# PSUM's eight banks shared out as three, three and two in place of four, two and two, in a Fourier and maxout kernel

## The chip, the cores and the metric

The kernel runs on one core of a Trainium2 chip. The metric is the device time of one execution in microseconds (us); lower is better. The kernel before was run three times; the profile is of one more execution, taken by the hardware profiler. Engines are named as the profile does: PE (TensorE), DVE (VectorE), ACT (ScalarE), POOL (GpSimd) and SP (SyncE, which here issues DMAs).

## The reference

A Fourier transform along the sequence, a complex matrix product, a soft threshold, the inverse transform, and then a layer that takes the largest of three products per token.

```python
def _attn_ref(x, w_r, w_i, b_r, b_i):            # x: (8, 3072, 256)
    X = np.fft.rfft(x, axis=1)
    Yr = X.real @ w_r - X.imag @ w_i + b_r
    Yi = X.real @ w_i + X.imag @ w_r + b_i
    Yr = np.sign(Yr) * np.maximum(np.abs(Yr) - 0.01, 0.0)
    Yi = np.sign(Yi) * np.maximum(np.abs(Yi) - 0.01, 0.0)
    return np.fft.irfft(Yr + 1j * Yi, n=3072, axis=1)

def _moe_ref(x, w1, w2, w3, w_out):              # x: (24576, 256), w1..w3: (256, 768)
    h = np.maximum(np.maximum(x @ w1, x @ w2), x @ w3)
    return h @ w_out                              # (24576, 256)
```

## The kernel before

**Precision.** A float32 operand is held as two float16 halves, high and low, and a product is three float16 matmuls into the same PSUM tile (`mm3`, lines 132, 133 and 134). Batch 0 alone goes through the Fourier part in float32.

**The Fourier part of a batch** turns 3072 points into 48 x 64. `stage_a` (L437) makes two PSUM tiles `pa`, which ACT copies out (L439) and a DMA writes to DRAM (`a_d`). After a reload (`aj`), `stage_b` makes one tile `px` per step; ACT and DVE read it (L127, L552, L553). `stage_w1` and `stage_w2` make one tile `py` each, the product with the complex weights, read by ACT (L631) and DVE (L620). `stage_q` makes `pz`, which ACT copies (L675) and a DMA writes to DRAM (`z_d`). Each of these steps is done 12 times per batch, `stage_a` 8 times.

**The inverse** of a chunk of 384 tokens (`inverse`, L735) reads `z_d` back and makes two tiles `pi`, which ACT and DVE split into the halves `yh` and `yl` (L127).

**The layer** works chunk by chunk (8 chunks per batch) and in six steps `f` per chunk. The weights are rearranged so that only two up products are needed: `up` makes two PSUM tiles `pu` of 128 x 384, each from six matmuls; ACT takes the ReLU of the first (`c`, L757), DVE the larger of that and the second (`h`, L759), and ACT and DVE split it into the halves of `hh` (L127). `down` (lines 132 to 134 into `pd`, from `hh`) multiplies by the output weights, nine matmuls per step. The part of the third product goes in through a product of weights (`wsh`, `wsl`). Two tiles `pd` take the sums of all six steps; ACT copies them out (L786).

**The order of the work.** The main loop at the end of `fourier_maxout_kernel` issues `up(f)`, then `down` of the step before, then what `run_until` has due of the next batch's Fourier part; with `f == 4` comes `inverse` of the next chunk. So PE's order around any step is: two tiles `pu`, `down` of the step before, some Fourier tiles, two tiles `pu`, and so on. PE, ACT and DVE each take their instructions in the order in which they stand. A scheduler may move instructions when the program is built: it knows how many buffers each pool has.

**PSUM.** It has eight banks, and each PSUM tile is one bank. A tag names a pool of banks: a new tile with the tag can be written when an earlier tile of the tag has been read for the last time. Before, `ff` had four banks, `up` two and `dn` two. All Fourier, inverse and small tiles come from `ff_tile`; from the main loop on, they all have the tag `ff` (`spare` is cut to one entry). Before the main loop, when no up or down products run, `ff_tile` takes tags from the list `spare` in turn, so that all eight banks serve the Fourier part of batch 0. `pu` has the tag `up` (L749) and `pd` the tag `dn`.

Of the kernel before, what the change touches and what calls it, by code (L numbers as in the profile page):

```python
# [9 lines left out]
F32 = mybir.dt.float32  # L10
# [86 lines left out]
def fourier_maxout_kernel(  # L97
# [5 lines left out]
    P = 128  # L103
# [14 lines left out]
    ps = ctx.enter_context(tc.tile_pool(name="ps", bufs=3, space=PSUM))  # L118
# [6 lines left out]
    def split_scaled(hi, lo, src, scale):  # L125
        h = hi if hi.dtype == F16 else hi.bitcast(F32)
        return nc.scalar.activation(out=hi, in_=src, func=AF.Copy, scale=scale), nc.vector.scalar_tensor_tensor(  # L127
            out=lo, in0=src, scalar=scale, in1=h, op0=ALU.mult, op1=ALU.subtract
        )

    def mm3(o, lh, ll, rh, rl, start=True, stop=True, **kw):
        nc.tensor.matmul(o, lh, rh, start=start, stop=False, **kw)  # L132
        nc.tensor.matmul(o, lh, rl, start=False, stop=False, **kw)  # L133
        nc.tensor.matmul(o, ll, rh, start=False, stop=stop, **kw)  # L134


    spare = ["ff", "up", "ff", "dn"]

    def ff_tile(name):
        tag = spare[0]  # L140
        if len(spare) > 1:
            spare.append(spare.pop(0))
        return ps.tile([P, 512], F32, name=name, tag=tag, bufs=4 if tag == "ff" else 2)

    fr = const.tile([XR, 64], F32, name="fr")
    qf = const.tile([P, 2, P], F32, name="qf")
# [50 lines left out]
    def exponent_of(mx, name, bits, mask, low):  # L197
        rows = mx.shape[0]
        col = small("col", bufs=2)
        nc.vector.tensor_reduce(out=col[0:rows], in_=mx, axis=AX.X, op=ALU.max)  # L200
        pt = ff_tile("pt")
        nc.tensor.matmul(
            pt[:, 0:rows], col[0:rows].broadcast_to([rows, P]), id_sb[0:rows, 0:rows],
            start=True, stop=True,
        )
        e = small("e" + name, U32, 2)
        nc.vector.tensor_reduce(out=e.bitcast(F32), in_=pt[:, 0:rows], axis=AX.X, op=ALU.max)
        nc.vector.tensor_scalar(
            out=e, in0=e, scalar1=bits, scalar2=mask, op0=ALU.logical_shift_right, op1=ALU.bitwise_and
        )  # L210
        nc.vector.tensor_scalar(out=e, in0=e, scalar1=low, scalar2=None, op0=ALU.max)
        return e
# [53 lines left out]
    class Weights:  # L266
# [27 lines left out]
        def phases(self, n):  # L294
# [32 lines left out]
            def turn():  # L327
                pt = ff_tile("pt")
                for j in range(width // P):
                    for v, first in ((m, True), (r, False)):  # L330
                        nc.tensor.matmul(
                            pt[:, j * P:j * P + P], v[:, j * P:j * P + P], id_sb, start=first, stop=not first
                        )
                pv = pt[:, 0:width].rearrange("p (f d) -> p f d", d=P)
                nc.scalar.activation(out=hi, in_=pv, func=AF.Copy)
                nc.vector.tensor_tensor(out=lo, in0=pv, in1=hi, op=ALU.subtract)
# [24 lines left out]
    def straight():  # L361
        ps_m = ff_tile("pm")
        for kd in range(KD):
            for f in range(NF):
                lh, ll = (t[:, f, kd * P:kd * P + P] for t in (wth, wtl))
                mm3(ps_m[:, kd * D:kd * D + D], lh, ll, woh[:, f], wol[:, f], start=f == 0, stop=f == NF - 1)
        split_scaled(*(t.rearrange("p k d -> p (k d)") for t in (wsh, wsl)), ps_m, H_SCALE)
# [320 lines left out]
    for q in range(NCH + 2, NB * NCH):  # L688
        b, i = divmod(q, NCH)
        p = i if b == 1 else (b - 2) * SLOTS + NF * i + 2  # L690
# [3 lines left out]
    for b in range(1, NB):  # L694
        for k in range(-2, NJP + 1):
            p = 8 + 2.2 * (k + 2) if b == 1 else (b - 1) * SLOTS + 2.8 * (k + 2)
# [49 lines left out]
    def up(y, f):  # L746
        pu = []
        for i in range(2):
            p = ps.tile([P, 512], F32, name="pu", tag="up", bufs=2)  # L749
            for kd in range(KD):  # L750
                mm3(
                    p[:, 0:NT], wuh[:, i, kd, f * P:(f + 1) * P], wul[:, i, kd, f * P:(f + 1) * P],
                    y[0][:, kd], y[1][:, kd], start=kd == 0, stop=kd == KD - 1,
                )
            pu.append(p[:, 0:NT])
        c1 = ffn.tile([P, NT], F32, name="c1")
        nc.scalar.activation(out=c1, in_=pu[0], func=AF.Relu)  # L757
        h32 = ffn.tile([P, NT], F32, name="h32")
        nc.vector.tensor_tensor(out=h32, in0=pu[1], in1=c1, op=ALU.max)  # L759
        hh = ffn.tile([P, 2, NT], F16, name="hh", bufs=4)  # L760
        st["hh"] = split_scaled(hh[:, 0], hh[:, 1], h32, H_SCALE)
        return hh
# [94 lines left out]
    for b in range(NB):  # L857
        for c in range(NCH):
            nxt = (b, c + 1) if c + 1 < NCH else (b + 1, 0) if b + 1 < NB else None
            for f in range(NF):  # L860
                hh = up(y, f)
                if prev:
                    down(*prev)
                prev = (b, c, f, hh, y)
                if b == c == 0:
                    for _ in range(5):
                        pump()
                    if f == 2:
                        split_fft_weights(fft_weights)
                    if f == 4:  # L870
                        straight()
                    if f in (3, 5):
                        for i in (f - 3, f - 2):
                            load_blocks(i)
                if nxt and f == 4:
                    y_next = inverse(*nxt)
                run_until(b * SLOTS + c * NF + f)
                if nxt and f == 1:
                    load_z(*nxt)
                    behind = st["hh"]  # L880
                if nxt and f == 3:
                    with tc.issue_after(behind[0].ins), tc.issue_after(behind[1].ins):
                        split_z(nxt[0])
            y = y_next
# [34 lines left out]
```

## Time and profile before

| | |
|---|---|
| three runs | 1828.95, 1829.1 and 1826.92 us; median 1828.95 us |
| profiled execution | 1830.64 us, of which the span from first to last instruction is 1828.8 us |
| busy over the span | PE 97%, DVE 71%, ACT 52%, POOL 7% |
| granted TensorE clock, mean | 0.997 |
| PE busy, 0 to 46 us | 22.7 us |
| PE busy, 46 to 200 us | 136.4 of 154 us |
| PE busy, 200 to 1829 us | 197 to 199 of every 200 us, 223.3 of the last 229 us |

The 0.0 of all times is the first instruction. Up to about 135 us the kernel loads and does the Fourier part of batch 0 while the weights are split; then the layer runs for 64 chunks, beside the Fourier part of the batch after. A row of the timeline gives start, duration, engine, line, operation and tiles (out<-in), and in brackets how long the engine was idle before and what ended that. Matmuls are pipelined: a `pu` matmul starts 0.16 us after the one before it, but its row says 0.33 us, and a `pd` matmul starts after 0.11 us and its row says 0.27 us. So idle time counts from an end that lies about 0.16 us behind the start of the next possible matmul, and a short wait shows no idle time at all.

### The profile page before, as it was taken

What the parts mean: (1) busy time and instruction counts of PE and PEld (TensorE: products, weight loads), DVE (VectorE), ACT (ScalarE), POOL (GpSimd) and SP (SyncE); (2) the same over time, 40 slices, a digit from 0 to 9 for tenths busy, and PEclk for the clock granted to TensorE, in tenths of its full rate; (3) what the DMA queues carried; (4) which work ended last, traced back from release to release, by engine and by line L of the source; (5) the groups of instructions that cost most, each with busy time, mean ns of one, the idle gap of its engine ahead of it and who ended that gap; (6) DMA issues with size and microseconds to landing.
All of it is one profiled execution on the core that took longest, in us unless ns stands there. A gap on an engine that the chain in (4) does not pass through costs nothing.

```text
span 1828.8 us, 39424 instructions
## 1 busy us (share of the span) xinstructions
PE 1766.7 (97%) x16071; PEld 1259.3 (69%) x16071; DVE 1303.5 (71%) x2580; ACT 954.6 (52%) x1930; POOL 130.1 (7%) x183
## 2 busy tenths in 40 slices
PE   4979999999999999999999999999999999999999
PEld 2755677767676777667677677766766677777776
DVE  1897789767886688757886588866888568864443
ACT  2335565555554556455554565545555455544443
POOL 0001100100000000100001000010001000000000
PEclk9999999999999999999999999999999999999999
DMA  8634433233323232232322333223232212211110
GB/s 247 221 116 120 126 93 88 72 111 91 94 66 103 86 94 84 69 117 77 96 82 70 113 90 91 78 70 115 86 96 67 87 53 73 64 36 54 40 36 27
DMA packets 116600, 164.71 MB, mean 90 GB/s; under 512 B 13137, under 2 KB 88914, under 8 KB 116418
## 3 DMA queue, kind: packets, MB, share of 16 engines
q1 hardware_dynamic: 54466, 86.66, 16.7%
q10 hardware_dynamic: 61952, 75.52, 13.6%
q8 instruction: 126, 2.06, 0.5%
q14 instruction: 56, 0.46, 0.1%
HBM read 86.64 MB, written 75.50 MB: 89 GB/s over the span
## 4 chain that ended last, share of the span: by engine, by line
PE 67%; DVE 13%; ACT 7%; DMA 6%; issue 4%; ACTq 2%; SPq 1%; POOL 0%; DVEq 0%; POOLq 0%
PE pu L132 10%; PE pu L134 10%; PE pu L133 10%; PE pd L134 7%; PE pd L133 6%; PE pd L132 6%; PE pa L437 3%; DVE u L620 3%; DVE h L759 2%; PE pi L735 2%; PE py L132 2%; PE py L134 2%; PE py L133 2%; DMA aj<-a_d 2%; ACTq L787 2%
## 5 line engine op out<-in xcount | busy, mean ns | idle before, releaser
L132 PE MATMUL pu<-yh,wuh 128*128 128x384 f16 x1536 | 501.5, 327 | 13.0 <-DVE h L759 7.1
L134 PE MATMUL pu<-yh,wul 128*128 128x384 f16 x1536 | 500.9, 326 | 0.0
L133 PE MATMUL pu<-yl,wuh 128*128 128x384 f16 x1536 | 500.8, 326 | 0.0
L127 ACT ACTIVATE hh<-h 128x384 f16<-128x384 f32 x384 | 200.6, 522 | 383.7 <-DVE h L759 376.2
L759 DVE TENSOR_TENSOR h<-pu,c 128x384 f32<-128x384 f32 x384 | 212.9, 554 | 162.5 <-PE pu L134 87.9
L134 PE MATMUL pd<-woh,hh 128*128 128x256 f16 x1152 | 313.9, 273 | 4.2 <-DVE hh L127 4.2
L132 PE MATMUL pd<-woh,hh 128*128 128x256 f16 x1152 | 313.9, 273 | 0.9 <-ACT hh L127 0.6
L133 PE MATMUL pd<-wol,hh 128*128 128x256 f16 x1152 | 313.9, 273 | 0.0
L127 DVE SCALAR_TENSOR_TENSOR hh<-h,hh 128x384 f16<-128x384 f32 x384 | 213.6, 556 | 122.0 <-ACT hh L127 120.8
L757 ACT ACTIVATE c<-pu 128x384 f32<-128x384 f32 x384 | 187.0, 487 | 129.4 <-PE pu L134 120.8
L132 PEld LDWEIGHTS <-wuh 128*128 128x128 f16 x1536 | 150.2, 98 | 115.0 <-issue 32.5
L133 PEld LDWEIGHTS <-wuh 128*128 128x128 f16 x1536 | 150.1, 98 | 102.4 <-issue 20.9
L134 PEld LDWEIGHTS <-wul 128*128 128x128 f16 x1536 | 150.1, 98 | 99.3
L620 DVE SCALAR_TENSOR_TENSOR u<-py,s1x,cs 64x256 f32<-64x256 f32 x308 | 148.4, 482 | 40.3 <-ACT cs L631 35.7
L132 PE MATMUL py<-wch,tt 128*128 128x256 f16 x504 | 137.7, 273 | 0.0
L134 PE MATMUL py<-wch,tt 128*128 128x256 f16 x504 | 137.4, 273 | 0.0
L133 PE MATMUL py<-wcl,tt 128*128 128x256 f16 x504 | 137.4, 273 | 0.0
L711 POOL MEMSET zp<- 32x1024 f32 x64 | 60.3, 943 | 1073.2 <-DVE zl L127 1029.4
L133 PEld LDWEIGHTS <-hh 128*128 128x128 f16 x1152 | 112.6, 98 | 31.5 <-issue 1.6
L132 PEld LDWEIGHTS <-hh 128*128 128x128 f16 x1152 | 112.7, 98 | 30.5 <-ACT hh L127 1.0
L134 PEld LDWEIGHTS <-hh 128*128 128x128 f16 x1152 | 112.6, 98 | 24.2 <-DVE hh L127 9.6
L786 ACT ACTIVATE o<-pd,s1u 128x256 f32<-128x256 f32 x192 | 83.1, 466 | 62.0 <-PE pu L134 35.4
(184 smaller groups left out, 2936.2 us busy)
## 6 DMA issues: line engine op xcount, KB each, us to landing
aj<-a_d SPq DMA_DIRECT2D x96, 256.0 KB, 2.8
z_d<-zs ACTq DMA_DIRECT2D x96, 256.0 KB, 2.2
zp<-z_d SPq DMA_DIRECT2D x128, 192.0 KB, 3.0
out_dram<-o ACTq DMA_DIRECT2D x192, 128.0 KB, 2.3
a_d<-aq ACTq DMA_DIRECT2D x124, 192.0 KB, 3.1
xq<-in_x_dram SPq DMA_DIRECT2D x120, 192.0 KB, 3.3
rw<-in_moe_w_dram SPq DMA_DIRECT2D x12, 384.0 KB, 7.5
xr<-in_x_dram SPq DMA_DIRECT2D x16, 96.0 KB, 3.8
```

The source lines that it names most:

```text
L127: return nc.scalar.activation(out=hi, in_=src, func=AF.Copy, scale=scale), nc.vector.scalar_tensor_tensor(out=lo, in0=src, scalar=scale, i ...
L132: nc.tensor.matmul(o, lh, rh, start=start, stop=False, **kw)
L133: nc.tensor.matmul(o, lh, rl, start=False, stop=False, **kw)
L134: nc.tensor.matmul(o, ll, rh, start=False, stop=stop, **kw)
L437: nc.tensor.matmul(pa[r][64 * c:64 * c + 64], fr[rows], xs[c][rows], start=True, stop=True)
L620: nc.vector.scalar_tensor_tensor(out=u[64 * c:64 * c + 64, j], in0=pk[r], scalar=inv[r], in1=c1[r], op0=ALU.mult, op1=ALU.add,)
L711: nc.gpsimd.memset(zq[32:64], 0.0)
L735: nc.tensor.matmul(pi[p][:, o:o + N1], lz[r, n2, h * P:(h + 1) * P], ga_sb[r, lg, c * NQ + n2, :], start=lz is zh and lg == 0, stop=lz is zl,)
L757: nc.scalar.activation(out=c1, in_=pu[0], func=AF.Relu)
L759: nc.vector.tensor_tensor(out=h32, in0=pu[1], in1=c1, op=ALU.max)
L786: nc.scalar.activation(out=o, in_=pd[t], func=AF.Copy, scale=st[b, "su"][1])
L787: nc.scalar.dma_start(out=out_v[b, c, t], in_=o)
```

## The change

The tag `up` gets three banks in place of two, and `ff` three in place of four; `dn` keeps two. The list `spare` now deals the eight banks to batch 0's Fourier part in the proportion three, three, two.

```diff
-    spare = ["ff", "up", "ff", "dn"]
+    spare = ["ff", "up", "dn", "ff", "up", "ff", "up", "dn"]
 
     def ff_tile(name):
         tag = spare[0]
         if len(spare) > 1:
             spare.append(spare.pop(0))
-        return ps.tile([P, 512], F32, name=name, tag=tag, bufs=4 if tag == "ff" else 2)
+        return ps.tile([P, 512], F32, name=name, tag=tag, bufs=2 if tag == "dn" else 3)
...
-            p = ps.tile([P, 512], F32, name="pu", tag="up", bufs=2)
+            p = ps.tile([P, 512], F32, name="pu", tag="up", bufs=3)
```

No instruction is added or taken away; the scheduler moves some. On PE, at six places some 217 us apart (one in a batch, from 532 us on), after an inverse and a tile `py`, a tile `pz` (Fourier) stood ahead of the first tile `pu` of the step. This is the difference there, PE's own order, with the weight loads (LDWEIGHTS, named by what is loaded) between the matmuls:

```order
 L134 LDWEIGHTS tt
 L134 MATMUL py<-wch,tt 128x256
+L132 LDWEIGHTS wuh
+L132 MATMUL pu<-yh,wuh 128x384
+L133 LDWEIGHTS wuh
+L133 MATMUL pu<-yl,wuh 128x384
+L134 LDWEIGHTS wul
+L134 MATMUL pu<-yh,wul 128x384
 L132 LDWEIGHTS qh
 L132 MATMUL pz<-vp,qh 128x512
```

The first three matmuls of the tile `pu` now stand ahead of `pz`, and its other three behind it. From 320 us on, PE's order is otherwise as it was; at 313 us a tile `px` in the same way goes behind a whole tile `pu`.

Ahead of 200 us more is moved, on PE, DVE, ACT and SP. The place that matters below is the first inverse (`pi`), on PE. Before, it followed the tiles `pa` of batch 1 directly (`pt` are small tiles for transposed weights, `rw`, and for scales, `col`):

```order
L331 MATMUL pt<-id_sb,rw 128x128 x6
L437 MATMUL pa<-xq,fr 64x512
L527 MATMUL pz<-uf,qf 128x256 x2
L437 MATMUL pa<-xq,fr 64x512
L202 MATMUL pt<-id_sb,col 128x128
L437 MATMUL pa<-xq,fr 64x512 x6
L735 LDWEIGHTS zh
```

Now there is more between, PE again:

```order
L437 MATMUL pa<-xq,fr 64x512
L202 MATMUL pt<-id_sb,col 128x128
L437 MATMUL pa<-xq,fr 64x512 x6
L331 MATMUL pt<-id_sb,rw 128x128 x6
L202 MATMUL pt<-id_sb,col 128x128 x2
L437 MATMUL pa<-xq,fr 64x512
L735 LDWEIGHTS zh
```

Six transposing matmuls, two for scales and one of `pa`, which before stood inside or behind the inverse, now stand ahead of it.

## The prediction

> **What bounds the kernel now.** I read the page first, then the waits of PE after 200 us, then PE's timeline at those waits. The page:
>
> ```profile
> span 1828.8 us, 39424 instructions
> PE 1766.7 (97%) x16071; PEld 1259.3 (69%) x16071; DVE 1303.5 (71%) x2580; ACT 954.6 (52%) x1930; POOL 130.1 (7%) x183
> ```
>
> PE is busy for 97% of the span: it is the bound, and a change can only win time in which PE waits, and can lose time wherever it makes PE wait. This is the whole answer on what PE waits for from 200 us to the end (us in total, times, longest):
>
> ```profile
> PE pu L132 <- DVE h L759: 6.6, 12, 0.8
> PE pu L132 <- ACT c L757: 5.5, 12, 1.2
> PE pd L134 <- DVE hh L127: 3.5, 14, 0.5
> PE pd L132 <- ACT hh L127: 0.6, 1, 0.6
> PE pd L132 <- ACT o L786: 0.3, 1, 0.3
> ```
>
> Two things are to be seen. The first two rows are the two `up` banks: a new tile `pu` waits until DVE or ACT has read the tile two before. They come to 12.1 us in 24 waits, and since each hides some 0.17 us behind the modelled end of the matmul before (a row of 0.33 us, a step of 0.16 us), to about 12.1 + 24 x 0.17 = 16.2 us. And there is no row for `pa`, `px`, `py`, `pz` or `pi`: with four banks no Fourier or inverse tile ever waits for a reader there.
>
> **Part 1: what the third `up` bank takes away.** With three banks a tile `pu` waits for the reader of the tile three before, which is a whole `down` and a tile earlier; I take all 16.2 us of these waits as gone. But the wait goes to whatever is late next. PE, ACT and DVE at a pair of such waits:
>
> ```profile
> 981.66 0.47 ACT L757 ACTIVATE c<-pu 128x384 f32<-128x384 f32 x1
> 982.18 0.32 PE L132 MATMUL pu<-yh,wuh 128*128 128x384 f16 x1 [0.31 <-ACT c L757]
> 983.37 0.55 DVE L759 TENSOR_TENSOR h<-pu,c 128x384 f32<-128x384 f32 x1
> 983.97 0.32 PE L132 MATMUL pu<-yh,wuh 128*128 128x384 f16 x1 [0.65 <-DVE h L759]
> 984.50 0.56 DVE L127 SCALAR_TENSOR_TENSOR hh<-h,hh 128x384 f16<-128x384 f32 x1 [0.59 <-ACT hh L127]
> 985.16 0.27 PE L134 MATMUL pd<-woh,hh 128*128 128x256 f16 x1
> ```
>
> The two tiles of this step wait for `c` and `h` of the step before. Behind them in PE's queue stands `down` of that same step, whose third matmul (L134) needs the low half of `hh`, the end of the very chain `c`, `h`, `hh`. DVE ends it at 984.50 + 0.56 = 985.06, and PE uses it at 985.16. A hand-over takes 0.05 (983.37 + 0.55 = 983.92, PE starts at 983.97). So without the two waits PE would stand at `down` and wait there: 0.05 us is won of some 1.3 us. DVE doesn't run earlier for it: it has the tile `pu` of this chain long before, and is held by its own queue. The other kind of place leaves more:
>
> ```profile
> 1028.63 0.32 PE L132 MATMUL pu<-yh,wuh 128*128 128x384 f16 x1 [0.62 <-ACT c L757]
> 1029.76 0.56 DVE L127 SCALAR_TENSOR_TENSOR hh<-h,hh 128x384 f16<-128x384 f32 x1 [0.59 <-ACT hh L127]
> 1030.80 0.27 PE L134 MATMUL pd<-woh,hh 128*128 128x256 f16 x1
> ```
>
> Here `hh` is there at 1030.32 and used at 1030.80: 0.43 us can be won. I count one such place in each of seven batches and twelve of the first kind: 7 x 0.43 + 12 x 0.05 = 3.6 us. The bounds are 0 (all of it reappears at `hh`) and 16.2 us (none does); I take 3.6, since the rows at the waits themselves give it.
>
> **Part 2: what the missing `ff` bank adds.** With three banks a Fourier or inverse tile waits for the last reader of the tile three before it, and PE takes nothing else while it waits. What is queued behind is everything, `up` and `down` first. Tiles that follow each other closely are in danger: two tiles `pi` and then `py` twice, or `py`, `py`, `pa`. In one batch I find four such places. The first two:
>
> ```profile
> 906.85 1.01 DVE L127 SCALAR_TENSOR_TENSOR yl<-pi,yh 128x384 f16<-128x384 f32 x2
> 907.09 0.27 PE L132 MATMUL py<-wch,tt 128*128 128x256 f16 x1
> 933.04 0.59 ACT L439 ACTIVATE aq<-pa 112x512 f32<-112x512 f32 x1
> 933.47 0.22 PE L735 MATMUL pi<-ga_sb,zh 48*128 48x48 f16 x4
> 935.50 0.27 PE L132 MATMUL py<-wch,tt 128*128 128x256 f16 x1
> 936.31 1.02 DVE L127 SCALAR_TENSOR_TENSOR yl<-pi,yh 128x384 f16<-128x384 f32 x2
> ```
>
> At 907.09 the second `py` would need the bank of the first `pi`, which DVE has read at about 906.85 + 0.53 = 907.38: with the hand-over, 0.35 us. At 933.47 the second `pi` needs the bank of `pa`, read by 933.63: 0.2 us. Two tiles later the second `py` at 935.50 needs the first `pi`, which DVE starts to read only at 936.31, behind `h` and `hh`, and has read at about 936.85: PE goes on at 936.90, 1.4 us late with the 0.2 in it. The other two:
>
> ```profile
> 958.65 1.09 PE L437 MATMUL pa<-xq,fr 48*64 48x512 f32 x8
> 959.31 0.42 DVE L553 SCALAR_TENSOR_TENSOR s<-px,s 128x256 f32<-128x256 f32 x1
> 964.70 1.02 DVE L127 SCALAR_TENSOR_TENSOR yl<-pi,yh 128x384 f16<-128x384 f32 x2 [0.94 <-ACT yh L127]
> 964.74 0.38 PE L132 MATMUL pz<-vp,qh 128*128 128x512 f16 x1
> 965.38 0.33 PE L132 MATMUL pu<-yh,wuh 128*128 128x384 f16 x1
> 965.87 0.33 PE L132 MATMUL pu<-yh,wuh 128*128 128x384 f16 x1
> ```
>
> At 958.65 `pa` needs the bank of a `px` that DVE has read at 959.73: 1.15 us. At 964.74 `pz` needs the first `pi`, read at 965.23, 0.55 us later; but here the new order puts three `pu` matmuls ahead of it, 965.87 - 965.38 = 0.49 us of work, so 0.05 us is left. One batch: 0.35 + 1.4 + 1.15 + 0.05 = 2.95 us. Of the tiles before and after, none has a reader as late. The place repeats in five batches: 14.8 us.
>
> The Fourier part of batch 1 is packed closer (events 2.2 apart in place of 2.8):
>
> ```profile
> 306.36 1.09 PE L437 MATMUL pa<-xq,fr 48*64 48x512 f32 x8
> 306.92 0.97 DVE L620 SCALAR_TENSOR_TENSOR u<-py,s1x,cs 64x256 f32<-64x256 f32 x2
> 312.60 0.22 PE L132 MATMUL px<-mb_all,ah 128*128 128x128 f16 x1
> 315.01 1.01 DVE L127 SCALAR_TENSOR_TENSOR yl<-pi,yh 128x384 f16<-128x384 f32 x2
> ```
>
> `pa` at 306.36 needs `py`, read at 307.89 (1.6 us), and `px` at 312.60 needs the first `pi`, read at about 315.55. The new order puts a whole tile `pu` ahead of it (six matmuls, 0.97 us), so PE is 315.6 - 313.6 = 2.0 us late there, with the 1.6 in it, since DVE's queue sets the time. I find two more of about 1.4 us at 215 and 245 us and two small ones, and take 5.0 us for batch 1 in all (bounds 2.0 and 6). Batch 7 has three places of 0.3 to 0.6 us, 1.5 us. Part 2 is 14.8 + 5.0 + 1.5 = 21.3 us. Its bounds: half of it, if ACT and DVE use each wait to get ahead and are less late at the next place; and 27, if none of the waits overlap.
>
> **Part 3: before the main loop.** The new order puts nine matmuls ahead of the first inverse, into a gap:
>
> ```profile
> 134.16 0.26 PE L735 MATMUL pi<-ga_sb,zh 48*128 48x48 f16 x4 [5.36 <-ACT zh L127]
> 105.00:120.00 15.00, 13.50 (x64) 10.78 (x63) 15.00 (x36) 7.27 (x15) 0.54 (x3) 1.00 0.33 103
> 135.00:150.00 15.00, 15.00 (x125) 10.15 (x125) 14.39 (x37) 8.35 (x19) 0.95 (x1) 0.83 0.13 42
> ```
>
> The two lower rows are windows (length, then busy us and count of PE, PEld, DVE, ACT and POOL, granted clock, DMA share, GB/s). PE idles 5.36 us there, but DVE is busy for all of 105 to 120 us and 14.4 of 15 us after 135, with the same work before and after the change. So I count 1.5 us won, and bound it by 4 us won (most of the gap) and 4 us lost (tiles `px` that now come in a row wait for their data; such a gap exists already).
>
> **The sum.** 1830.6 - 3.6 + 21.3 - 1.5 = 1846.8 us for an execution like the profiled one. That one is 1.7 us above the median of the runs shown, so I predict 1846.8 - 1.7, about 1845 us, 0.9% slower. A measurement of this kernel can tell about 0.2% (3.7 us) from no change.
>
> **A page that speaks against the change.** The windows show what waits do to the clock: after the gap of 5.36 us the granted clock is 0.83 over 15 us, while a window of 15 us that holds a wait of 1.2 us on `pu` keeps 1.00:
>
> ```profile
> 760.00:775.00 15.00, 13.12 (x98) 8.51 (x96) 12.32 (x22) 6.45 (x13) 1.91 (x2) 1.00 0.09 28
> ```
>
> So I charge nothing for the clock. The Trainium skill, "TensorE: Matmul & The Clock Gate", section "A second HAM failure mode: psum-queue depth-cycling", says otherwise: in a kernel that cycled through its PSUM banks, small idle times between groups of matmuls made the clock swing between half and full rate. By that rule the added waits would cost more than their length; this trace doesn't bear it out for waits of up to 1.2 us.
>
> **The rivals.**
> - *The third bank pays in full* (chance 0.1). If ACT and DVE get through `c`, `h` and `hh` earlier because `pu` is there earlier, all of the 16.2 us is won: 1845 - 12.6 = about 1832 us, 0.2% slower. For it: ACT is half idle. Against it: the rows at 982 to 985, where DVE is busy from 983.37 on and `hh` comes 0.1 us before its use.
> - *Faster: the readers move up* (0.07). At each place of part 2 DVE stands at `h` and `hh` of the layer before it comes to the tile of the inverse. If with the third bank that layer work is done a step earlier, the reads of `pi` and `px` move ahead; it decides from about 1.1 us earlier on, when places such as 958.65 cost nothing. Then part 2 falls to some 4 us and part 1 pays in full: 1829 - 16.2 + 4 - 1.5 = about 1815 us. Against it: `h` can't be earlier than its second tile `pu`, which PE makes just ahead.
> - *The waits add up* (0.1): 27 us in part 2, nothing won in part 1 and 4 lost in part 3: 1829 + 31 = 1860 us.
> - *The clock falls* (0.03): with some 17 waits of over 1 us, each followed by a window like that from 135 to 150 us (0.17 of 15 us, 2.6 us), 44 us more: about 1889 us.
>
> **How the numbers follow.** The forecast has the remaining 0.7; its own range, from the bounds of part 2 and part 3, is 1835 to 1855. To hold the time 8 times in 10 the range takes in the first rival at 1832 and most of the way to the third: 1832 to 1858. Faster by over 0.2%: the second rival, 0.07. Within 0.2%: half of the first rival and a little of the forecast's low end, 0.08. Slower: 0.85.
>
> **What would show it.** In the profile after, the rows of `pu` waiting for `h` and `c` should be gone or under 1 us, and those of `pd` waiting for `hh` longer than 4.1 us. New rows should stand for `py`, `pa`, `px` and `pi` waiting for DVE or ACT, some 15 us after 200 us, at the places named. Wrong would be: no such rows, waits of `hh` as before with `pu`'s gone, or a granted clock under 0.99 after 200 us.

## The result and the profile after

The changed kernel takes 1838.87 us (median of 4 runs, 1837.99 to 1840.39), the kernel before 1828.76 us (4 runs, 1826.92 to 1829.1). The ratio is 1.0058, with an interval of 1.0041 to 1.0076: some 10 us slower. The profiled executions stand 7.4 us apart (1838.07 and 1830.64 us), since that of before lay above its median and that of after below its own.

The page after, span and engines:

```profile
span 1836.3 us, 39429 instructions
PE 1776.0 (97%) x16071; PEld 1260.2 (69%) x16071; DVE 1305.6 (71%) x2580; ACT 956.9 (52%) x1930; POOL 130.8 (7%) x183
```

PE is still busy for 97%. The five instructions more in the first row are none of the five engines' counted work: those counts are as before. What PE waits for from 200 us on (us in total, times, longest):

```profile
PE py L132 <- DVE yl L127: 6.6, 11, 1.1
PE pd L132 <- ACT hh L127: 5.3, 7, 1.1
PE pd L134 <- DVE hh L127: 5.1, 22, 0.3
PE py L132 <- DVE s L553: 2.0, 3, 1.3
...
PE px L132 <- DVE yl L127: 0.4, 1, 0.4
...
```

Two changes are to be seen. The rows of `pu`, 12.1 us before, are gone; the rows of `pd` for `hh` have grown from 4.1 to 10.4 us. And `py` and `px`, which never waited for a reader before, now wait 9.0 us for `yl` and `s`.

To see where the time is lost, the same instruction is followed in both kernels: the first matmul of one tile `pu` near 200 us, of one near 320 us (end of batch 1's Fourier part) and of one near the end. Before:

```profile
197.84 0.33 PE L132 MATMUL pu<-yh,wuh 128*128 128x384 f16 x1
318.82 0.33 PE L132 MATMUL pu<-yh,wuh 128*128 128x384 f16 x1
1782.42 0.33 PE L132 MATMUL pu<-yh,wuh 128*128 128x384 f16 x1
```

And the same three after the change:

```profile
194.52 0.32 PE L132 MATMUL pu<-yh,wuh 128*128 128x384 f16 x1
320.13 0.33 PE L132 MATMUL pu<-yh,wuh 128*128 128x384 f16 x1
1789.62 0.33 PE L132 MATMUL pu<-yh,wuh 128*128 128x384 f16 x1
```

The changed kernel leads by 3.3 us at the first (194.52 - 197.84), is 1.3 us behind at the second, and 7.2 us behind at the third. So 3.3 us are won ahead of 200 us, 4.6 us lost in batch 1 and 5.9 us in batches 2 to 7.

The places in one batch that the prediction named, after the change:

```profile
910.01 0.27 PE L132 MATMUL py<-wch,tt 128*128 128x256 f16 x1 [0.20 <-DVE yl L127]
...
936.04 0.43 PE L735 MATMUL pi<-ga_sb,zh 48*128 48x48 f16 x4
...
938.89 1.01 DVE L127 SCALAR_TENSOR_TENSOR yl<-pi,yh 128x384 f16<-128x384 f32 x2
...
939.50 0.27 PE L132 MATMUL py<-wch,tt 128*128 128x256 f16 x1 [1.05 <-DVE yl L127]
...
961.92 0.42 DVE L553 SCALAR_TENSOR_TENSOR s<-px,s 128x256 f32<-128x256 f32 x1
962.12 1.40 PE L437 MATMUL pa<-xq,fr 48*64 48x512 f32 x8
```

All the waits are where they were expected. The second `py` at 910.01 waits for the first `yl`. The first group of `pi` takes 0.43 us in place of 0.22: the second tile waits 0.2 us. The second `py` at 939.50 stands still until DVE is halfway through `yl` (938.89 + 0.53 = 939.42). But `pa` is another matter. Before, it began at 958.65, ahead of the read `s` at 959.31; now that read begins ahead of it, at 961.92, and `pa` is only stretched by 1.40 - 1.09 = 0.31 us. PE came later to `pa` by 962.12 - 958.65 = 3.47 us, DVE to `s` by only 2.61 (2.58 at 938.89): the stall at 939 held PE and not DVE, so at the next place the read had already begun when PE came.

The place where `pu` waited for `c` and `h` of the step before, and a `pu` matmul some steps ahead of it:

```profile
969.74 0.33 PE L132 MATMUL pu<-yh,wuh 128*128 128x384 f16 x1
...
986.63 0.68 DVE L656 TENSOR_REDUCE mxu<-u 128x1 f32<-128x512 f32 x1
987.23 0.55 DVE L759 TENSOR_TENSOR h<-pu,c 128x384 f32<-128x384 f32 x1
...
988.36 0.56 DVE L127 SCALAR_TENSOR_TENSOR hh<-h,hh 128x384 f16<-128x384 f32 x1 [0.59 <-ACT hh L127]
988.39 0.28 PE L132 MATMUL pd<-woh,hh 128*128 128x256 f16 x1 [0.70 <-ACT hh L127]
...
988.98 0.28 PE L134 MATMUL pd<-woh,hh 128*128 128x256 f16 x1 [0.20 <-DVE hh L127]
```

No tile `pu` waits here any more; `pd` waits for the high half of `hh` and then for the low half. The matmul at 969.74 stood at 965.87 before, 3.87 us earlier; the one at 988.98 stood at 985.16, 3.82 us earlier. The two waits taken away between them have won 0.05 us. DVE takes `h` directly behind `mxu`, a Fourier instruction: the third bank has not made the chain `c`, `h`, `hh` any earlier. It has only moved the place at which PE meets it.

### The profile page after: what moved, and what is told of

It is laid out like the page before. It is cut to its first block, busy times and chain, and to the rows that moved or that the text cites. A ratio compares the mean times of both kernels' runs of the same rounds, so it can differ in the third digit from the quotient of the medians.

```text
span 1836.3 us, 39429 instructions
## 1 busy us (share of the span) xinstructions
PE 1776.0 (97%) x16071; PEld 1260.2 (69%) x16071; DVE 1305.6 (71%) x2580; ACT 956.9 (52%) x1930; POOL 130.8 (7%) x183
## 4 chain that ended last, share of the span: by engine, by line
PE 66%; DVE 15%; ACT 7%; DMA 5%; issue 4%; ACTq 2%; SPq 0%; POOL 0%; DVEq 0%; POOLq 0%
PE pu L132 10%; PE pu L134 9%; PE pu L133 9%; PE pd L134 7%; PE pd L132 7%; PE pd L133 7%; PE pa L437 3%; DVE h L759 3%; DVE u L620 3%; PE py L132 2%; PE pi L735 2%; PE py L133 2%; PE py L134 2%; DVE hh L127 1%; ACT zh L127 1%
## 5 line engine op out<-in xcount | busy, mean ns | idle before, releaser
L132 PEld LDWEIGHTS <-hh 128*128 128x128 f16 x1152 | 112.8, 98 | 40.0 <-ACT hh L127 11.4
L134 PEld LDWEIGHTS <-hh 128*128 128x128 f16 x1152 | 112.6, 98 | 28.7 <-DVE hh L127 13.7
```

## The experiments

The theory after the result: the lost `ff` bank costs about 12 us, the third `up` bank returns almost nothing since its waits go to `hh`, and something ahead of 200 us wins some 3 us. The rival: the third bank does pay, and the change loses for another reason (the dealing of banks to batch 0, or the order that the scheduler makes of it). Each kernel was timed beside the kernel before on the same chip; kernels that ran on different chips are compared by their ratios to it.

**One bank less for `ff` alone.** The eighth bank serves only batch 0, ahead of the main loop.

```diff
-    spare = ["ff", "up", "ff", "dn"]
+    spare = ["ff", "up", "ff", "dn", "ff", "up", "one", "dn"]
-        ... bufs=4 if tag == "ff" else 2)
+        ... bufs={"ff": 3, "one": 1}.get(tag, 2))
```

> Fourier and inverse tiles with three banks, up products with two as before, one bank unused in the main loop; before the main loop all eight banks are dealt out in the proportion of before. Theory (an up wait only moves to the low half of hh, and the lost fourth bank costs some 1 to 1.5 us a batch net): about 1842 us (1838 to 1846), with waits of pu back at some 12 us and waits of py for yl as in the changed kernel. Rival (the third up bank pays in full, 16 us, and the fourth Fourier bank was worth 26): about 1855 us.

Measured: 1841.62 us, ratio 1.0064 (1.005 to 1.0078), 11.8 us over the kernel before on that chip, as the theory said. What PE waits for most from 200 us on:

```profile
PE py L132 <- DVE yl L127: 6.6, 11, 1.1
PE pu L132 <- ACT c L757: 5.8, 13, 0.6
PE pu L132 <- DVE h L759: 4.2, 7, 0.7
PE py L132 <- DVE s L553: 3.0, 4, 1.3
```

The waits of `py` are those of the changed kernel, while `pu` still waits as before, 10.0 in place of 12.1 us. The missing `ff` bank alone makes the kernel slower by as much as the whole change. This kernel starts the tile of the first landmark at 197.10 and that of the third at 1792.66 us: it leads by 0.7 us at the first and is 10.2 us behind at the third, 11.0 us lost after 200 us. The changed kernel loses 3.3 + 7.2 = 10.5 us there. Three `up` banks in place of two are worth next to nothing after 200 us.

**The new dealing of banks alone.** Batch 0 gets its banks in the proportions of the changed kernel; the main loop has four, two and two.

```diff
-    spare = ["ff", "up", "ff", "dn"]
+    spare = ["ff", "up", "dn", "ff", "one", "ff", "up", "dn"]
...
-    del spare[1:]
-    spare[0] = "ff"
+    spare[:] = ["ff", "ff", "ff", "one"]
```

> Before the main loop the banks are dealt out as in the changed kernel; in the main loop four, two and two as before. Theory (the changed kernel won 3 to 4 us ahead of 200 us and lost it in the main loop): about 1826 us (1823 to 1829), no wait of py for yl. Rival (what is lost lies in the new order before the main loop and at its start): about 1837 us.

Measured: 1830.44 us, ratio 1.0006 (0.9995 to 1.0017). The theory's 1826 us is missed, and the rival's 1837 us too: the dealing wins nothing and loses nothing.

**The old dealing with the new sharing.** The main loop is that of the changed kernel; batch 0 gets its banks in nearly the old order.

```diff
-    spare = ["ff", "up", "dn", "ff", "up", "ff", "up", "dn"]
+    spare = ["ff", "up", "ff", "dn", "ff", "up", "up", "dn"]
```

> Before the main loop the banks are dealt out in the proportion of before; in the main loop three, three and two as in the changed kernel. Theory: the changed kernel without its gain ahead of 200 us, about 1842 us (1839 to 1845). Rival (the loss lies before the main loop): about 1830 us.

Measured: 1837.99 us, ratio 1.0038 (1.0023 to 1.0054). Both are missed, the theory's 1842 and the rival's 1830 us. With the old dealing it starts the tile of the first landmark at 194.01 us, 3.8 us ahead of the kernel before. This table puts the landmarks of the traces together (us against the kernel before; minus is ahead):

| kernel | `up` banks, first chunks | `ff` banks after | at 198 | at 319 | at 1782 |
|---|---|---|---|---|---|
| after | 3 | 3 | -3.3 | +1.3 | +7.2 |
| old dealing, new sharing | 3 | 3 | -3.8 | +0.8 | +7.6 |
| three `up` banks early only (below) | 3 | 4 | -2.9 | -1.5 | -0.1 |
| one `ff` bank less | 2 | 3 | -0.7 | +3.8 | +10.2 |
| new dealing alone | 2 | 4 | +0.5 | +0.3 | -1.3 |

These are single executions, and the stretch ahead of 200 us varies: PE's first long wait, for the DMA of `aj`, ends between 38.8 and 40.7 us in the thirteen traces of this document. Still, the lead at 198 us goes with the third `up` bank, whatever the dealing. Of the other kernels below, four with three `up` banks lead by 1.9 to 6.6 us there and one (`pi` in the pool of `up`, `down` two behind) lies at +0.1; the two with two `up` banks lie at +0.2 and -0.6. In time this bank is worth 1841.62 - 1837.99 = 3.6 us on one chip. Whether it wins through shorter waits of the first chunks or through the order that the scheduler makes of them isn't told apart by these runs.

**Three `up` banks only where they win.** The third bank belongs to `up` for the first two chunks, then to `ff`. `ff_tile` and the first dealing are as in "One bank less for `ff` alone"; the rest of the edit:

```diff
+    up_tags = ["up", "up", "one"]
...
+            tag = up_tags[0]
+            up_tags.append(up_tags.pop(0))
-            p = ps.tile([P, 512], F32, name="pu", tag="up", bufs=2)
+            p = ps.tile([P, 512], F32, name="pu", tag=tag, bufs=1 if tag == "one" else 2)
...
+            if b == 0 and c == 2:
+                up_tags[:] = ["up", "up"]
+                spare[:] = ["ff", "ff", "ff", "one"]
```

> The kernel before, but for the first two chunks the up products have three banks and the Fourier tiles three; from the third chunk on (about 200 us) two and four. Theory, formed after the runs so far (the third up bank is worth some 3.5 us, all of it ahead of 200 us, where DVE splits weights): a lead of about 3 us at 200 us that stays, 1826 us (1824 to 1828). Rival (that lead comes from the order that the scheduler makes with three banks throughout, or is given back in the next chunks): 1829 to 1831 us.

Measured: 1828.1 us against 1831.14 on that chip, ratio 0.998 (0.997 to 0.999): 3.0 us faster, the gain that the theory named; in microseconds it lies between the two ranges. The profiled execution, the slowest of the ten at 1830.74 us, shows the rival's picture: its lead of 2.9 us is worn down to 0.1 us by 1782 us, and its span is that of the kernel before. So a gain is measured, but that it is the lead at 198 us, kept to the end, is not shown.

**`down` two steps behind `up`, on the changed kernel.** If the waits for `hh` are what the third bank's gain went into, more room ahead of `down` must bring it out.

```diff
-    prev = None
+    behind_down = []
...
-                if prev:
-                    down(*prev)
-                prev = (b, c, f, hh, y)
+                behind_down.append((b, c, f, hh, y))
+                if len(behind_down) > 2:
+                    down(*behind_down.pop(0))
...
-    down(*prev)
+    for step in behind_down:
+        down(*step)
```

> The changed kernel with down two steps behind up in place of one, so that hh has a whole step more; all else as it is, same work. Theory (the third up bank is worth nothing because down, one step behind, waits for the same chain): the waits of pd for hh, some 11 us in the list and 16 with what hides behind modelled ends, go, and the time falls to about 1825 us (1821 to 1830). Rival (DVE and ACT are behind on their work as a whole, so any wait removed comes back elsewhere): 1837 to 1840 us.

Measured: 1826.8 us, ratio 0.9981 (0.997 to 0.9991), 0.77% or 14 us under the changed kernel, as the theory said. What PE waits for most from 200 us on:

```profile
PE py L132 <- DVE s L553: 6.5, 9, 1.5
PE py L132 <- DVE yl L127: 1.2, 5, 0.2
```

All waits for `hh` are gone. Those of `py` for Fourier readers, the price of the `ff` bank, are still there, now for `s` more than for `yl`.

**The same on the kernel before.** The same edit. The theory: two `up` banks leave the waits of `pu`, so it gains less. The rival: it pays by itself.

> The kernel before (four, two, two) with down two steps behind up; same work. Theory (with two up banks the chain of c and h holds pu itself, so moving down back frees only the waits for hh): the waits of pu stay at some 12 us in the list, those of pd for hh (4 us) go, 1825 us (1822 to 1829), and the step that was worth 12 us in the changed kernel is worth 3 to 6 us here. Rival (the later down pays by itself, whatever the banks): the same 12 us as in the changed kernel, about 1818 us.

Measured: 1815.49 us (1814.45 to 1815.89), ratio 0.9909 (0.9894 to 0.9924), 15.7 us faster than before: the rival is right, by more than the 12 us it named, and no version is faster. What PE waits for from 200 us on, the two rows of `pu`:

```profile
PE pu L132 <- DVE h L759: 4.2, 8, 1.0
...
PE pu L132 <- ACT c L757: 0.3, 1, 0.3
```

Not only `hh`'s rows are gone; those of `pu` fell from 12.1 to 4.5 us with two banks as before. But `down` is not all that moved: here, and in the version above, the scheduler also gives DVE and ACT another order. At the place of the prediction's first pair of waits `zl` (980.91) and `vp` (982.11) stood ahead of `h` (983.37) on DVE. The same `h` in this kernel:

```profile
973.18 0.56 DVE L759 TENSOR_TENSOR h<-pu,c 128x384 f32<-128x384 f32 x1 [1.41 <-ACT c L757]
...
976.00 0.74 DVE L127 SCALAR_TENSOR_TENSOR vp<-u,s0v,vp 128x512 f16<-128x512 f32 x1
...
977.12 1.28 DVE L127 SCALAR_TENSOR_TENSOR zl<-zp,s0u,zh 112x1024 f16<-112x1024 f32 x1
```

Now both stand behind it, and on ACT `c` and `hh` come ahead of `zh` and `vp` in the same way. So this run has two causes in one, more room for `hh` and an earlier place for the readers in their queues. The second suggests that the two `up` banks were hardly short. The next two runs test it without moving `down`.

**The chain first, on the kernel before.** Two Fourier steps that need not be early, the split of `v` (`vp`) and the maximum of `u` (`mxu`), are held back on DVE until `hh` of the step is done.

```diff
+            with tc.issue_after(st["hh"][1].ins):
                 split_scaled(*st["v", k], u, st[b, "sv"][0])
...
+        with tc.issue_after(st["hh"][1].ins) if b else nullcontext():
             st["max"] = nc.vector.tensor_reduce(
```

> The kernel before, with DVE and ACT holding back the split of v (vp) and the maximum of u (mxu) until hh of the step is split; nothing else changed. Theory, formed after the run with down two steps behind (PE waits for c, h and hh because Fourier work stands ahead of them in the order of DVE and ACT): the waits of pu for h and c fall from 12 us to 4 to 8, those of pd for hh too, about 1824 us (1820 to 1828). Rival (the sum of DVE's work at these places sets the time, in whatever order): within 2 us of before, 1828 to 1832 us.

Measured: 1825.96 us against 1830.1, ratio 0.9977 (0.9968 to 0.9985), 4.1 us faster with no bank moved; the theory's range held. DVE at the place of the prediction's first pair of waits, before:

```profile
980.91 1.28 DVE L127 SCALAR_TENSOR_TENSOR zl<-zp,s0u,zh 112x1024 f16<-112x1024 f32 x1
...
982.77 0.68 DVE L656 TENSOR_REDUCE mxu<-u 128x1 f32<-128x512 f32 x1
```

And the same place with the chain first (its lines from there on are numbered two higher):

```profile
979.36 1.28 DVE L127 SCALAR_TENSOR_TENSOR zl<-zp,s0u,zh 112x1024 f16<-112x1024 f32 x1
...
980.61 0.56 DVE L761 TENSOR_TENSOR h<-pu,c 128x384 f32<-128x384 f32 x1
...
983.42 0.74 DVE L127 SCALAR_TENSOR_TENSOR vp<-u,s0v,vp 128x512 f16<-128x512 f32 x1
```

Before, `h` came at 983.37, 2.46 us behind the start of `zl`; now it comes 1.25 us behind it. What PE waits for most from 200 us on:

```profile
PE pu L132 <- ACT c L759: 8.0, 13, 1.3
PE pd L134 <- DVE hh L127: 3.7, 12, 0.5
PE pu L132 <- DVE h L761: 1.7, 3, 0.8
```

Those for `h` fall from 6.6 to 1.7 us; those for `c` rise from 5.5 to 8.0. On ACT `vp` still stands ahead of `c` (980.10):

```profile
979.48 0.72 ACT L127 ACTIVATE vp<-u,s0v 128x512 f16<-128x512 f32 x1
```

So the waits fell less than the theory said: those of `pu` to 9.7 us in place of 4 to 8, and those of `pd` for `hh`, with a row of 0.5 us for ACT, not at all (4.2 after 4.1).

**The chain first, on the changed kernel.** The same edit.

> The changed kernel with the same two operations held back behind hh. Theory: the waits of pd for hh (11 us in the list) fall by a third to two thirds, those of py for yl stay, about 1832 us (1828 to 1836). Rival (DVE's sum of work sets the time): 1837 to 1841 us.

Measured: 1831.97 us, ratio 1.0009 (1.0 to 1.0017), 0.49% or 9 us under the changed kernel, as the theory said. What PE waits for most:

```profile
PE py L132 <- DVE yl L127: 8.1, 12, 1.3
PE pd L134 <- DVE hh L127: 3.8, 13, 0.5
```

The waits for `hh` are down from 10.4 to 3.8 us, those of `py` for the `ff` bank do not fall (8.1 after 6.6). So most of the waits at `hh` come from what stands ahead of the chain on DVE.

**A bank of `up` for the second `pi`, with `down` two behind.** The tile whose bank `py` waits for moves to the pool that has one to spare.

```diff
-        pi = [ff_tile("pi") for _ in range(2)]
+        pi = [ff_tile("pi"), ps.tile([P, 512], F32, name="pi", tag="up", bufs=3)]
```

> The changed kernel with down two steps behind, and the second of the two inverse tiles takes a bank of the up products in place of a Fourier bank. Theory (py waits for the reading of pi because two of the three Fourier banks hold pi): the waits of py for yl go and those for s shrink, 4 to 6 us less than with down two steps behind alone, about 1822 us (1819 to 1825). Rival (pi in the up pool makes pu wait for DVE, which reads pi late): 1827 to 1832 us, with waits of pu for yl.

Measured: 1816.12 us, ratio 0.9912 (0.9898 to 0.9925), 0.69% under the version without this edit and level with the fastest. Of the rows of `py`, 7.7 us without it, one is left:

```profile
PE py L132 <- DVE s L553: 1.2, 1, 1.2
```

So with `down` two behind, nearly all that the `ff` bank costs is in where `pi` lies: the ratio is that of four `ff` banks, 0.9909. The theory had the direction, but too small a size (1822 us).

**The same, with `down` one behind:** the line of `pi` above, on the changed kernel.

> The changed kernel, but the second inverse tile takes a bank of the up products; down one step behind as in the changed kernel. Theory (what the change loses is the waits of py for a bank that holds pi, 8 to 10 us with what hides behind modelled ends): those waits go, about 1831 us (1828 to 1834). Rival (PE only trades them for waits of pu or pd, since DVE is as late as before): 1836 to 1840 us.

Measured: 1837.42 us, ratio 1.0039 (1.0026 to 1.0052); its interval overlaps that of the changed kernel. The theory's 1831 us is missed. The two largest waits:

```profile
PE pd L134 <- DVE hh L127: 7.6, 26, 0.8
PE pd L132 <- ACT hh L127: 6.1, 9, 1.2
```

`py` no longer waits for `yl`, which took 6.6 us, and PE waits for `hh` for 13.7 us in place of 10.4, for `o` for 2.7 in place of 0.4. The rival is right: with `down` one step behind, most of the wait taken away ahead of it comes back at `down`.

**Both gains together: three `up` banks early, and `down` two behind, on the kernel before.**

> The kernel of the third up bank in the first two chunks, four and two after, with down two steps behind. Theory: both gains add, the kernel before with down two steps behind less 3.5 us, about 1822 us (1818 to 1826). Rival (down two behind already hides what the third bank wins in the first chunks): no difference between the two.

Measured: 1815.81 us, ratio 0.9912 (0.9899 to 0.9926), the same as with `down` two behind alone. The 3 us of the early bank don't add. They are not hidden in the first chunks, as the rival has it: the profiled execution leads by 6.6 us at 198 us, the one with `down` two behind alone is 0.2 us behind there; by 1782 us the two are only 2.0 us apart.

## Why the prediction was right in direction and wrong in size

It said 1845 us, slower, with a range of 1832 to 1858; measured were 1838.87. The mechanism is the one forecast: the 12.1 us of `pu` waits are gone, the waits for `hh` have grown by 6.3, and there are new waits for the missing `ff` bank. For the profiled execution it summed to 16.2 us; the profiles show 7.4, the medians 10.1. Some of the errors have opposite signs: part 2 was too large, part 1 found a gain where there is none, and part 3 was too small.

*Part 1, the third `up` bank (3.6 us won).* That the wait moves to `hh` was right: at 982 to 985 the two waits are gone and 3.87 - 3.82 = 0.05 us is won, the figure forecast. (The trace before has six such pairs, not twelve; at 0.05 us each this weighs little.) What failed is "0.43 us can be won", taken as a gain that stays. It read `hh` at 1030.32 and its use at 1030.80 as slack. After the change:

```profile
1033.78 0.56 DVE L127 SCALAR_TENSOR_TENSOR hh<-h,hh 128x384 f16<-128x384 f32 x1 [0.59 <-ACT hh L127]
...
1034.39 0.28 PE L134 MATMUL pd<-woh,hh 128*128 128x256 f16 x1 [0.20 <-DVE hh L127]
...
1037.77 0.28 PE L134 MATMUL pd<-woh,hh 128*128 128x256 f16 x1 [0.20 <-DVE hh L127]
```

DVE ends the low half of `hh` at 1034.34, 4.02 us later than before, and PE uses it at 1034.39, only 3.59 us later: the slack is used up, and 0.43 us is won at the place. But one step on PE waits for the next `hh`, which DVE ends 4.02 us later as well: the matmul at 1037.77 stood at 1033.79 before, 3.98 us earlier, so the gain is gone again. The 3.6 us that the bank does bring (one chip, table above) lie ahead of 200 us, where this part didn't look; after 200 us the two kernels with the bank lose 10.5 and 11.4 us, the one without 11.0.

*Part 2, the missing `ff` bank (21.3 us lost).* This is the term that was mis-sized: taking the bank alone costs 11.8 us, near the lower bound named, "half of it, if ACT and DVE use each wait to get ahead". Batch 1 was right (5.0 forecast; 4.6 by the landmarks). Batches 2 to 7 were to lose 14.8 + 1.5 - 3.6 = 12.7 us and lost 5.9. In the batch shown, the waits of `py` and `pi` came at their size: 0.2 at `pi`, and at `py` 1.05 us of idle time beside the 0.17 hidden. Two things were not in the sum. The 1.15 us at `pa` became 0.31, because the stall at 939 had made PE later and DVE not. And a stall for an `ff` tile takes the place of the next wait. The lag of PE behind the kernel before is 2.92 us at 907.09 and down to 2.57 at a tile `pu` (926.04 before), which waited 0.19 us for `h` before and now finds it read. It grows to 4.00 at 935.50 and is back at 3.47 by `pa`, since it falls by 0.17 at a `pu` (954.94 before) and by 0.33 at a `pd` that waited for `hh` (956.47 before). The third `up` bank has no part in that: with one `ff` bank less and two `up` banks the lag falls at the same places, from 4.29 to 3.95 and from 5.36 to 4.85. The forecast let each `pu` wait reappear at `hh` and added the `ff` waits on top; one stretch of time was charged twice.

*Part 3, ahead of the main loop (1.5 us won).* The gain by 198 us is 3.3 us, but the reason was wrong. The nine matmuls do go into the gap: PE now waits 3.78 us there, for the data `xq` of a moved `pa`, in place of 5.36. But the kernels with the new dealing alone and with one `ff` bank less make the same move; their first tile `pu` starts 0.6 us earlier and 0.8 us later than before, and at 198 us they lie at +0.5 and -0.7. The old dealing with three `up` banks makes it too and leads by 3.8 us. So the move does not bring the lead. In the changed kernel the first tile `pu` starts 4.1 us earlier (135.07 against 139.21); why more than in the others is not shown.

*The clock.* Nothing was charged, rightly for the main loop. After the change (columns as in the prediction; the 1.00 is the granted clock):

```profile
320.00:1780.00 1460.00, 1441.92 (x13502) 1029.62 (x13501) 1046.79 (x2018) 783.48 (x1581) 105.96 (x152) 1.00 0.27 80
```

The rule of the Trainium skill that the prediction weighed, "TensorE: Matmul & The Clock Gate", section "A second HAM failure mode: psum-queue depth-cycling", is not seen here for waits of this length: the row is 1.00 over the 1460 us that hold nearly all of them, the longest of 1.1 us. Ahead of 200 us, and in one of the other kernels, it is otherwise (last section).

*The rivals.* "The third bank pays in full" falls with the waits for `hh`, which grew by 6.3 us. "The readers move up" falls with `yl`, which still comes too late for `py`. "The waits add up" falls with the lags above: they replace each other.

What stays open is how much of the 15.7 us of `down` two behind comes from room for `hh` and how much from the other order on ACT and DVE. Holding `vp` and `mxu` back on DVE moved 4.1 us; the rest was not taken apart. Open too is how the third `up` bank wins its 3 us ahead of 200 us.

## What to carry to other kernels

A PSUM bank takes away a wait only if the tile's reader isn't the start of a chain that the same engine needs a little later: read on along the chain to its last use, and look for what holds the reader in its own queue. Waits of one engine can't simply be added: here each stall left the other engines as early as they were, and so shortened the next wait. Before banks are moved between pools, try the distance between producer and consumer and the order in the readers' queues; here one more step of distance, with the other order that came with it, was worth 15.7 us, and the banks were worth -10.

## What the runs showed of the hardware that was not expected

A wait of PE can cost more than its length, and windows of 15 us hide it. Around a wait of 5.85 us for `col`, which ends at 97.32 in the changed kernel, and behind one of 2.48 us for a PSUM bank, the granted clock is:

```profile
94.00:97.30 3.30, 0.00 (x0) 0.00 (x0) 3.23 (x7) 0.00 (x0) 0.00 (x0) 0.50 0.47 135
97.30:100.70 3.40, 3.38 (x7) 2.17 (x8) 2.34 (x13) 1.59 (x4) 0.00 (x0) 0.50 0.02 5
100.70:105.00 4.30, 4.30 (x21) 3.78 (x21) 4.12 (x13) 2.95 (x7) 0.00 (x0) 0.99 0.36 122
...
159.23 0.48 PE L132 MATMUL pu<-yh,wuh 128*128 128x384 f16 x1 [2.48 <-DVE h L759]
159.00:162.20 3.20, 2.97 (x20) 1.53 (x20) 3.20 (x6) 1.43 (x3) 1.70 (x2) 0.50 0.65 173
```

The clock is at 0.50 for some 3.4 us behind the wait for `col` and for some 3 us behind the wait of `pu`, where PE is busy, and full again behind that. Half the clock over 3.4 us is about 1.7 us lost, an estimate from these rows. The prediction's rival on the clock charged 2.6 us behind such a wait: here that is too much, and nothing is too little. The runs give no length of wait from which this begins. In the changed kernel waits of up to 1.3 us after 200 us did not bring the clock down. But with `down` two steps behind on the changed kernel a `pa` waits only 0.75 us for `aq` (its row starts at 212.15), and behind it the clock falls as well:

```profile
213.00:216.40 3.40, 3.40 (x13) 1.46 (x12) 2.88 (x5) 1.68 (x3) 0.94 (x1) 0.51 0.59 158
```
